# New work orders for an attention and long-convolution kernel, with some layernorm rows on GpSimd and other residual additions on VectorE

## The chip, the cores and the metric

The kernel runs on one core of a Trainium2 chip. The metric is the device time of one execution in microseconds (us); times given as "the time" are the median of several executions. The engines of the core are named as in the profile: PE is TensorE (matmul), PEld its weight loads, DVE is VectorE, ACT is ScalarE, POOL is GpSimd, and SP only issues DMAs here.

## The reference

One sequence of 2048 positions and 512 features goes through four sublayers, A, B, A, B, each with a layernorm in front and its result added to the residual stream x. A is windowed, dilated attention with 32 heads of 16 features: a position attends to itself and to seven earlier positions, two apart. B is a long convolution of the sequence with a kernel of 2048 taps for each feature, which is generated from state-space parameters.

```python
def _A_ref(x, wqkv, wo):                       # H = 32, Dh = 16, W = 8, dil = 2
    ...
    idx = pos[:, None] - off[None, :]          # off = 0, 2, ..., 14
    ...
    logits = jnp.einsum("bhsd,bhswd->bhsw", q, kg) * scale
    logits = jnp.where(mask[None, None, :, :], logits, -1e9)
    attn = _softmax(logits, axis=-1)
    o = jnp.einsum("bhsw,bhswd->bhsd", attn, vg)
    return o.transpose(...).reshape(B, S, D) @ wo
def _B_ref(u, A_re, A_im, B_re, B_im, C_re, C_im, log_dt, Dskip):
    ...
    P = jnp.exp(logdA[:, :, None] * l[None, None, :])
    K = jnp.einsum("dn,dnl,dn->dl", Cc, P, dB).real
    ...                                        # y = irfft(rfft(u, 2L) * rfft(K, 2L))[:L]
    return y + u * Dskip
x = x + _A_ref(_layernorm(x), A_wqkv, A_wo)
x = x + _B_ref(_layernorm(x), B_A_re, ..., B_Dskip)
x = x + _A_ref(_layernorm(x), A_wqkv, A_wo)
x = x + _B_ref(_layernorm(x), B_A_re, ..., B_Dskip)
```

The convolution kernel depends on the parameters alone and serves both layers. In this program it is brought into a frequency domain once, and each convolution is then a chain of two forward steps, a multiplication, and two inverse steps, all as matmuls with small transform matrices.

## The kernel before

The 2048 positions are split into 16 rows of 128, row a holding every sixteenth position from a on; x stays in SBUF as x_sb, 128 partitions by 16 rows by 512 features, in bf16. There are seven stages, by time in the profile: kernel generation together with the first layernorm, its projections and the first logits (0 to 109 us); the core of attention 0 (109 to 187); convolution 0 (187 to 237); the second front, which is the end of convolution 0, the layernorm of layer 2 and its projections (237 to 270); the core of attention 1 (270 to 360); convolution 1 (360 to 408) with the stores of the output.

The order of the instructions of PE, DVE, ACT and SP is not left to a scheduler. It is written out by hand, as strings of tokens, under a manual schedule: each token calls a small function that emits its instructions, and each engine executes what it was given in this order, waiting on semaphores where an operand is not there yet or a buffer is not free. So to move a token is to move its work on every engine that it uses. Seven strings are concerned:

- ORDERK is the order of kernel generation: 368 one-letter tokens that build the powers of the state-space poles (L1106 on DVE), the transcendental functions of ACT, the matmuls that make the convolution kernel's taps (L1264, PE), and among them the front of attention 0.
- CORE0 and CORE1 are the orders of the two attention cores, read by `core`. The tokens: v is one step of the v projection (PE matmuls L396, copied to v_ext by ACT, L398; every few steps SP copies shifted rows of v_ext by DMA, L401 and L402), q of the q projection, m a product of q and k for a row's window (DVE, L340), l its sum over the features of a head (PE, L343 to L352), x the maximum (DVE, L412), e the exponentials (ACT, L424), r the reciprocals, n the normalised weights (DVE, L443 or L446), P the product of weights and v of a row (DVE, L465, output pav), S and V its sum over the window on PE. S adds halves of pav with 64 small matmuls of 64x64 (L490), V whole ones with 32 (L480). O is the output projection (PE, L499 to L501) and the update of x by ACT (L505 or L507). b, d and a belong to the layernorm in front of the convolution: statistics, 1/sqrt, and the application to one row (`u_apply`; L195 on DVE or POOL, L193 on ACT). Digits and other letters are events: loads of w2 and of transform data, and fix-ups of the convolution kernel.
- ORDER0 and ORDER1 are the orders of the convolutions. Each token makes one tile of 128x1024 or 128x2048 elements, and its last letter says which engine takes the result out of PSUM: A for ACT, D for DVE, B for half on each. K and U are the first forward step (f1, matmuls L798, taken out by L787) of the convolution kernel and of the sequence; k and u the second (f2, L805); m the multiplication on DVE (L848, L851); y and Y half and whole tiles of the first inverse step (i1, L878, L882); z and w tiles of the second (i2). A z tile covers four rows and 256 features, a w tile eight rows and 128 features, and a v tile four rows and 128 features.
- i2 adds its result to x. Where ACT takes the tile out, PE adds x itself, by one more matmul with the identity for each row (L905, L925). Where DVE does, it adds x while it reads PSUM (L910, L929).
- KROWS gives the engine, ACT or DVE, that takes out each K tile of the second half of the kernel. ORDERF is the order of the second front: the last tiles of convolution 0, h statistics of half rows (DVE, L148), a their aggregation (L1492), p the power for 1/sqrt (ACT), n the norms of four rows (L195), T the transposes of those rows (PE, L269), E their way out of PSUM (L271), P the projection for k (PE, L280), Q that for q (L221), x and e the copies of k's shifted edges (DVE, L293).

In the second front the norm of a block of four rows is one call, which before puts all four rows on DVE:

```
def norm(b):
    la.front_apply(b, x_sb[:, b * 4:(b + 1) * 4, :], ln_end(nc, lnp, ln[b]), ["dve"] * 4)
```

In the cores the engine that applies the norm to a row is fixed by the row's number: even rows from 0 to 7 on ACT, odd ones on DVE. In layer 1 rows 8 to 15 follow behind the core on POOL, which is not under the manual order outside of kernel generation; in layer 2 rows 8 and 9 are on ACT, 10 and 11 on DVE.

The outputs leave at the end by eight stores of four rows and 256 features each (L1535, on SP), each as soon as its part of x is final.

Of the kernel before, what the change touches and what calls it, by code (L numbers as in the profile page):

```python
# [45 lines left out]
ORDERK = """
sibCCiGCsibGCiMisibsbGcCiCMibabcsMMMTMGiiMTGMaTbaisiTMbbcTTsiaTGbibsTTaiiaTbbbcMsTGaiGMaMMiGMb
lMlaMGsGWiiaMalbMyyyyTMMaaiaMtMMweMtaMMMMedTaqcMMMslMkMaqlQkiqWKMbMqMlkyHyQTkyUkUkyKTtUqtKUUppaU
qaUaUUqUxaUqaQakapxUelQekdUlpUkWKkKHxkqTlT3Tky3qxKTT3pT3pTQylyqxTkWqylxQpTkKtpzzTqzeTkqHtkxQeKUU
zktkKkUEETkeUUktKTkkUkKTUUeKkkpkxpKUxkpUEUxUKkqUxUUUUpqoUkpoxKXUQxoUkpkKXZpxXxpxZZ  # L50
"""
ORDER0 = """
KD KD KA KA KA KD KA KA KD KA KD kA KD kA KD UA UA kD UA UA UD kA UD UA UA KD
kA kD u kD kA u UA m KD u u m UA m UD UD UA UA u m KA u u m UD kA
m u kD kA m kA kD kD UA kA u kA u m yA m u m yD yA u u m YA m m
u u m m yA u m yA yA YD yD yA YD yA yA z01D yD yA
# [123 lines left out]
def ln_end(nc, pool, st):  # L180
    rstd, mean, ms = st
    nb = pool.tile(list(rstd.shape), F32, name="ln_nb")
    nc.vector.scalar_tensor_tensor(nb[:], mean, ms, rstd[:], ALU.mult, ALU.mult)
# [7 lines left out]
def ln_apply(nc, out_ap, in_ap, rstd, nb, a, eng):  # L191
    if eng == "act":
        nc.scalar.activation(out_ap, in_ap, ACT.Identity, bias=nb[:, a:a + 1], scale=rstd[:, a:a + 1])  # L193
    else:
        (nc.gpsimd if eng == "pool" else nc.vector).tensor_scalar(out_ap, in_ap, rstd[:, a:a + 1], nb[:, a:a + 1], ALU.mult, ALU.add)  # L195
# [1179 lines left out]
def kernel(  # L1375
# [104 lines left out]
    with tc.manual_schedule(engines=MAN):  # L1480
        la.front_open()
        la.front_zero()
        ln, agg, pts = {}, {}, {}
# [4 lines left out]

        def aggr(b):
            agg[b] = lnp.tile([P, 4, 2], F32, name="ln_ag")  # L1490
            for a in range(4):
# [80 lines left out]
```

## Time and profile before

| | us |
|---|---|
| median of 3 executions (lowest, highest) | 411.57 (411.03, 413.31) |
| the profiled execution | 409.99 |
| its span | 408.2 |
| DVE, ACT, PE, POOL busy in the span | 381.0, 327.0, 322.2, 55.7 |

The span goes from the first to the last instruction or transfer of the profiled execution; 1.8 us lie around it. A timeline row gives the start, the duration, the engine, the line of the kernel, the operation, output<-inputs, shapes, and how many instructions were merged into the row; in brackets how long the engine stood idle before it and which engine's result ended that. On DVE an instruction starts some 0.09 us before the one in front of it is recorded as ended, so the step from start to start is the price in a full queue: 2.20 us for a pav of 2.29, 1.14 for a copy out of PSUM of 1.22.

### The profile page before, as it was taken

To read this page: it belongs to the slowest core of one execution; us is meant where nothing else is said; L and a number is where in the kernel's file an instruction comes from. 1 tells how busy PE (TensorE), PEld (TensorE's weight loads), DVE (VectorE), ACT (ScalarE), POOL (GpSimd) and SP (SyncE) were. 2 spreads that over 40 slices of the span, in tenths; PEclk is the share of its full clock that TensorE was granted. 3 is DMA by queue.
4 is the path that set the end of the run, shared out by engine and by line. 5 is a ranking of instruction groups with operands and counts; after the bars stand their busy time and mean duration, and the time that the engine had idled before them with its cause. 6 is when DMAs were issued, how large, how long until landed. Compare 5 with 4: busy or idle time off the path is not lost.

```text
span 408.2 us, 14705 instructions
## 1 busy us (share of the span) xinstructions
PE 322.2 (79%) x6467; PEld 226.9 (56%) x6513; DVE 381.0 (93%) x478; ACT 327.0 (80%) x562; POOL 55.7 (14%) x73
## 2 busy tenths in 40 slices
PE   3000259899899888888988889999998999897794
PEld 2000127567536565656877778544466676566783
DVE  6999999999999999998899989888989999989983
ACT  7999999896456599898999978865655758889972
POOL 9300500000499200101300000000000020000000
PEclk9999999999999999999999999999999999999998
DMA  7941822132015845583245486930043027505516
GB/s 219 395 120 20 92 68 72 33 64 70 14 43 138 242 127 178 157 340 107 80 160 193 172 305 139 334 106 2 0 117 92 3 86 330 158 3 156 160 29 181
DMA packets 62322, 54.17 MB, mean 133 GB/s; under 512 B 33869, under 2 KB 50738, under 8 KB 60978
## 3 DMA queue, kind: packets, MB, share of 16 engines
q1 hardware_dynamic: 62250, 53.22, 43.1%
q8 instruction: 51, 0.84, 0.9%
q14 instruction: 13, 0.11, 0.1%
q10 hardware_dynamic: 8, 0.00, 0.0%
HBM read 30.15 MB, written 13.24 MB: 106 GB/s over the span
## 4 chain that ended last, share of the span: by engine, by line
PE 36%; ACT 15%; DVE 13%; DMA 10%; issue 6%; SPq 4%; DVEq 0%; ACTq 0%
PE pq L396 5%; PE pk L1264 5%; DVE pav L465 4%; PE pp L1202 4%; DMA v_ext<-v_ext 3%; PE pq L221 3%; ACT a1s L787 3%; PE pp L280 3%; ACT ub L864 3%; DMA w_sb<-w_dram 2%; PE L L348 2%; PE pq L501 2%; DMA kf_ring<-kf_dram 2%; PE pb L882 2%; DVE prod L340 2%
## 5 line engine op out<-in xcount | busy, mean ns | idle before, releaser
L465 DVE TENSOR_TENSOR pav<-attn,v_ext 128x4096 bf16<-128x4096 bf16 (+1 forms) x34 | 73.1, 2168 | 1.4 <-DMA v_ext<-v_ext 0.8
L340 DVE TENSOR_TENSOR prod<-qT,kT_ext 128x4096 bf16<-128x4096 bf16 x29 | 67.1, 2339 | 1.6 <-ACT qT L223 1.1
L1106 DVE TENSOR_TENSOR A_t<-A_t,pow_t 128x1024 bf16<-128x1024 bf16 (+4 forms) x46 | 38.3, 875 | 0.3
L1192 PE MATMUL pt<-ident,x_blk 128*128 128x128 bf16 x64 | 6.3, 241 | 40.0 <-DMA w_dram<-w_q 38.5
L490 PEld LDWEIGHTS <-pav 64*128 64x128 bf16 x1664 | 26.3, 95 | 14.9 <-DVE pav L465 8.0
L490 PE MATMUL po<-ident,pav 64*128 64x64 bf16 x1664 | 29.0, 190 | 6.4 <-DVE pav L465 3.6
L501 PE MATMUL pq<-wop,oT 128*128 128x512 bf16 x122 | 31.6, 379 | 2.8 <-issue 1.9
L864 ACT CAST ub<-pb 128x1024 bf16<-128x1024 f32 x32 | 32.3, 1090 | 0.1
L398 ACT CAST v_ext<-pq 128x512 bf16<-128x512 f32 x32 | 18.8, 586 | 17.0 <-PE pq L396 16.0
L805 PE MATMUL pb<-a1s,w_sb 128*128 128x64 bf16 x768 | 28.0, 193 | 5.4 <-ACT a1s L787 2.3
L396 PE MATMUL pq<-wv,xnT 128*128 128x512 bf16 x121 | 30.1, 379 | 0.6 <-ACT kgs L1272 0.3
L1202 PE MATMUL pp<-xnT,kT_ext 128*128 128x512 bf16 x87 | 25.0, 404 | 6.9 <-ACT qT L1207 2.9
L805 PEld LDWEIGHTS <-w_sb 128*128 128x128 bf16 x768 | 25.0, 98 | 8.0 <-issue 5.2
L787 DVE CAST a1s<-pb 128x1024 bf16<-128x1024 f32 x21 | 25.0, 1219 | 4.1 <-PE pb L798 4.1
L1192 PEld LDWEIGHTS <-x_blk 128*128 128x128 bf16 x64 | 4.8, 108 | 42.4 <-ACT x_blk L193 41.0
L787 ACT CAST a1s<-pb 128x1024 bf16<-128x1024 f32 x27 | 26.4, 1052 | 2.3 <-PE pb L798 2.2
L1264 PEld LDWEIGHTS <-A_t 128*64 128x64 bf16 (+1 forms) x512 | 21.8, 103 | 4.1 <-issue 0.6
L1264 PE MATMUL pk<-B_t,A_t 128*64 128x84 bf16 (+1 forms) x512 | 23.6, 201 | 0.1
L221 PE MATMUL pq<-xnT,kT_ext 128*128 128x512 bf16 x89 | 22.8, 379 | 0.5 <-issue 0.3
L176 POOL TENSOR_TENSOR ln_rstd<-ln_rstd,ln_mh 128x4 f32<-128x4 f32 x2 | 3.9, 1971 | 125.5 <-DVE ln_rstd L175 125.5
L501 PEld LDWEIGHTS <-oT 128*128 128x128 bf16 x128 | 12.4, 98 | 14.2 <-ACT oT L492 1.3
L492 ACT CAST oT<-po 128x512 bf16<-128x512 f32 x26 | 15.0, 577 | 5.7 <-PE po L490 5.6
(259 smaller groups left out, 885.0 us busy)
## 6 DMA issues: line engine op xcount, KB each, us to landing
w_sb<-w_dram SPq DMA_DIRECT2D x8, 1024.0 KB, 6.4
w_dram<-xnT SPq DMA_DIRECT2D x1, 4096.0 KB
kf_ring<-kf_dram SPq DMA_DIRECT2D x13, 256.0 KB, 4.2
kf_ring<-kf_dram SPq DMA_DIRECT2D x26, 128.0 KB, 3.9
v_ext<-v_ext SPq DMA_DIRECT2D x4, 784.0 KB, 7.4
x_blk<-in_A_x_dram SPq DMA_DIRECT2D x4, 512.0 KB, 4.5
kT_ext<-in_A_wqkv_dram SPq DMA_DIRECT2D x4, 512.0 KB, 9.9
x_sb<-in_A_x_dram SPq DMA_DIRECT2D x4, 512.0 KB, 5.2
```

The lines of the kernel that those rows point to most:

```text
L221: nc.tensor.matmul(pq[:], lhsT=self.wqk[:, dt, ft * P:(ft + 1) * P], rhs=self.xnT[:, dt, q * 512:(q + 1) * 512], start=(dt == 0), stop=(dt ...
L340: nc.vector.tensor_tensor(pr, self.qT[q][:, ft].unsqueeze(1).to_broadcast([P, W, 4, P]), kap, ALU.mult)
L396: nc.tensor.matmul(pp[:], lhsT=xnT[:, dt, a * P:(a + 1) * P], rhs=wv[:, dt, :], start=(dt == 0), stop=(dt == NDT - 1))
L465: nc.vector.tensor_tensor(pv[:, i], attn[:, n % 4].unsqueeze(2).to_broadcast([P, W, DH // parts, H]), vap, ALU.mult)
L490: nc.tensor.matmul(po[:, h, 0, i * nt + ft, :], lhsT=pvf[rows, i, w, ft * P:(ft + 1) * P], rhs=ident[rows, rows], start=(w == 0 and ft + i ...
L501: nc.tensor.matmul(pw[:], lhsT=oT[:, ftp, :], rhs=self.wo[:, ftp, :], start=False, stop=(ftp == NDT - 1))
L787: (self.nc.scalar.copy if eng == "act" else self.nc.vector.tensor_copy)(dst, src)
L805: nc.tensor.matmul(p2[:, j, :], lhsT=self.w2[:, ec * EC + j, :], rhs=a1s[:, ec * EC + j, :], start=True, stop=True)
L864: nc.scalar.copy(ub[:], p2)
L1106: return lambda: nc.vector.tensor_tensor(*args)
L1202: nc.tensor.matmul(pps[kind, b, ft][:], lhsT=la.wqk[:, dt, c:c + P], rhs=la.xnT[:, dt, b * 512:(b + 1) * 512], start=(dt == 0), stop=(dt = ...
L1264: nc.tensor.matmul(o, lhsT=lhs, rhs=Bt[:, ri, c * CH + ql].rearrange("p b g -> p (b g)"), start=(not half and j % 4 == 0 and ri == 0), sto ...
```

## The change

All seven strings are new, and three of them change what is done where:

- ORDERK holds the same 368 tokens in another order.
- CORE0 has 13 S and 3 V instead of 15 and 1; CORE1 13 S and 3 V instead of 11 and 5. There are now two letters for the norm of a row, a on DVE and f on ACT: CORE0 has 6 a and 2 f where before 4 rows were on DVE and 4 on ACT; CORE1 has 4 a and 8 f where 6 were on ACT and 6 on DVE.
- In convolution 0, one K tile goes from DVE to ACT and one U tile from ACT to DVE; KROWS has the same counts in another order. One y tile goes from DVE to ACT. The last i2 tiles before were one on DVE and seven on ACT; now they are three on DVE, one on ACT and eight v tiles (half width) on ACT.
- In the second front, the norms of blocks 0, 1 and 2 put rows 0 and 2 on GpSimd and rows 1 and 3 on DVE, six rows on GpSimd in all; block 3 stays on DVE. Two E copies change sides.
- In convolution 1, one y tile goes from DVE to ACT; the i2 tiles of DVE go from two w, three z and a half z (of a tile shared with ACT) to two w, two z and five v; those of ACT from one z, a half z and two v to three v.

```diff
 ORDERK = """
-sibCCiCGCsibGCiMisibsbGcCiCMibabcsMMMTMGiiMTGMaTbaisiTMbbcTTsiaTGbibsTTaiiaTbbbcMsTGaiGMaMMiGMb
...
+sCiibsCbiisCiiMbMCGMiMsabiMcbiasMbbCCaGiMMTsibGGTGTicMbGsbiaTbcisbbTTTMGiiTbTiMaGsaGGTMiGacMabTl
...
 ORDERF = """
-yA z00A z10A h01 h00 h10 z11A a0 z12A h11 p0 S z02A n0 a1 z03A h02 p1 T0 E01D n1 h12 a2 E00A
-z13A P01 P02 T1 E11D E10A h03 Q00 p2 P00 n2 P03 h13 P10 P12 P11 T2 a3 E20A p3 E21D n3 P13 P23
-P20 P21 T3 E31D x1 E30A P22
+yA yA z01D yA z00D yA yD h00 yA h01 YA v100A v110A v102A v013A h10 a0 p0 n0G z02A v111A v101A S v112A
+h02 h11 T0 E00A a1 E01A z13D p1 n1G v003A P03 Q00 h12 a2 P01 T1 E10A p2 P00 E11D n2G h03 P11 P12
+P13 T2 E20A h13 a3 E21D P02 p3 n3D P22 P21 P10 T3 E30D E31D P23 P20 x1
 """
 ORDER1 = """
...
-yA yA yD YD yA YA yD z03D yD yA yA w000D yA yA w010D z02D v100A v110A z11A z12D z13B
...
+YA m yA YD w000D yA yA yD yA z03D yA w010D yA yD yA z02D v103A v113D v112D v102D v110D v100A v111D v101A
 """
 CORE0 = """
-vmvvv0lvmvqxleqqmlmvrlqmvvnTlmvvxlmevmlvvrlmvvlnTqPxSePS1qmOlPr4SO2PmqS3OlnP5SP67qmOSOlP8ASOPmPb
-BOSlCSwxdeOPaSaarPODVOPnbSOPd9SEOaaPaSOPGFaaPtOSHbSOt
+vvmvvlvmvvmlvxlemvrmnlqmqvlTvqlxevqmlvmvmPvvP1rnllxS0qTmqOeVmrqP4qSl2OPPSOSOPSmPP5On3l8ml6SPCOOV
+AlxSPP7eOSrObSPn9POSdOESOPSPbDadBPfaGOtFOaaawVfHSbatO
 """
 CORE1 = """
-0m1l2ml3mvmqqqqlmlvmvvvxlqmvleqlrqmqlnTvmvvxlemvmvlvrvlmvvvlPnSTxqePSOmlqPrVOqOPmSPlnSOPOmqSlPVO
-PmbVOPlxdaVeOrPawSOPaaVOPnbSOPdSOPaSOPPaatSObStadaaaaO
+0m1l2ml3mvvqqlmmlmvqqvvllxmemqvlrnvvlmxTqqlvvmqlmvPvvvvmvqlleqVPrmxqmnqSTOePlPmSOPllSPOSPrOSnOPS
+mOSPOblxOSPPdeOSrffbVPdfwOnPfVOPSOSPafbOPSdafftOSafatO
 """
-KROWS = "ADADADAA"
+KROWS = "ADDAADAA"
...
-            def u_apply(a0, rows, eng=None):
+            def u_apply(a0, rows, eng):
...
-                             eng or ("dve" if a % 2 else "act"))
+                    ln_apply(nc, u[:, :, a, :], x_sb[:, a, :].rearrange("p (q r) -> p q r", r=4), rstd, nb, a - a0, eng)
...
+            for key, eng in (("a", "dve"), ("f", "act")):
+                ops[key] = iter([lambda eng=eng: (lambda a: u_apply(a - a % 4, (a,), eng))(next(applied))] * 12)
...
-            eng = dict(A="act", D="dve", B="both").get(tok[-1])
+            eng = dict(A="act", D="dve", B="both", G="mixed").get(tok[-1])
...
-        def norm(b):
-            la.front_apply(b, x_sb[:, b * 4:(b + 1) * 4, :], ln_end(nc, lnp, ln[b]), ["dve"] * 4)
+        def norm(b, eng):
+            la.front_apply(b, x_sb[:, b * 4:(b + 1) * 4, :], ln_end(nc, lnp, ln[b]), dict(both=["act", "dve"], mixed=["pool", "dve"]).get(eng, [eng] * 2) * 2)
```

A token H for the statistics of four whole rows (`whole_stats`) comes with the change, but none of the orders uses it.

More of the change, by code (lines that the diff above doesn't have):

```diff
@@ L46 @@
 ORDERK = """
[L47 to L50, printed above, removed]
+sCiibsCbiisCiiMbMCGMiMsabiMcbiasMbbCCaGiMMTsibGGTGTicMbGsbiaTbcisbbTTTMGiiTbTiMaGsaGGTMiGacMabTl
+MlMMMWMlaiMsiMayMwMiMybyaTMysteMMqatMaaMkeMadTkqMialKMMlQMkWMlaqMMcbqykTQHqUaUKqQaakUTyqUkyqUUpU
+KUkyUapxUxtaUpatpeUaldHQqeUqkKUkl3TT33TQkkxpWl3KxTpTxyxTylTWTpqlkyyTqpHKkzkQzxKUtkUktezUqqeUKTkT
+kQKztktkTeeKkUkUKTTkkKUUUkUxUUpxEUpkxpUkUUkpEKkKqxpkUxoxpEoKXqUokUkQUpKxpZxXxZXZ
 """
 ORDER0 = """
[L53 to L56, printed above, removed]
+KD KA KA KA KD KA KD KA KD KA KD kA kD kA kA kD UA KD UA UD kA UA kD UA KD UA
+UD UA KD kA u UD m UA KA u UD u UD m KA u kA m m UA u u kD m m u
+UA u UD kA m UA kD kA u m kA kD u kA yA m YD m u m u YA u u m u
+yA m m u yA m m YA yA yD yD
 """
@@ L59 @@
 ORDERF = """
-yA z00A z10A h01 h00 h10 z11A a0 z12A h11 p0 S z02A n0 a1 z03A h02 p1 T0 E01D n1 h12 a2 E00A
-z13A P01 P02 T1 E11D E10A h03 Q00 p2 P00 n2 P03 h13 P10 P12 P11 T2 a3 E20A p3 E21D n3 P13 P23
-P20 P21 T3 E31D x1 E30A P22
+yA yA z01D yA z00D yA yD h00 yA h01 YA v100A v110A v102A v013A h10 a0 p0 n0G z02A v111A v101A S v112A
+h02 h11 T0 E00A a1 E01A z13D p1 n1G v003A P03 Q00 h12 a2 P01 T1 E10A p2 P00 E11D n2G h03 P11 P12
+P13 T2 E20A h13 a3 E21D P02 p3 n3D P22 P21 P10 T3 E30D E31D P23 P20 x1
 """
 ORDER1 = """
-UA UD UA UD UA UD UD UA UA UD UA u UD u u m u m m UA m u UD u m u
-UA m UA u u m m u m u m u yD m u yA yA m m u m u yA m u m
-yA yA yD YD yA YA yD z03D yD yA yA w000D yA yA w010D z02D v100A v110A z11A z12D z13B
+UA UD UA UD UA UA UD UA UD UA UD u UD u u UA m u m u m UA m u m u
+UD m m UA u m u m u u yA YA u m m u yD m YA m u u m m u yA
+YA m yA YD w000D yA yA yD yA z03D yA w010D yA yD yA z02D v103A v113D v112D v102D v110D v100A v111D v101A
 """
 CORE0 = """
-vmvvv0lvmvqxleqqmlmvrlqmvvnTlmvvxlmevmlvvrlmvvlnTqPxSePS1qmOlPr4SO2PmqS3OlnP5SP67qmOSOlP8ASOPmPb
-BOSlCSwxdeOPaSaarPODVOPnbSOPd9SEOaaPaSOPGFaaPtOSHbSOt
+vvmvvlvmvvmlvxlemvrmnlqmqvlTvqlxevqmlvmvmPvvP1rnllxS0qTmqOeVmrqP4qSl2OPPSOSOPSmPP5On3l8ml6SPCOOV
+AlxSPP7eOSrObSPn9POSdOESOPSPbDadBPfaGOtFOaaawVfHSbatO
 """
 CORE1 = """
-0m1l2ml3mvmqqqqlmlvmvvvxlqmvleqlrqmqlnTvmvvxlemvmvlvrvlmvvvlPnSTxqePSOmlqPrVOqOPmSPlnSOPOmqSlPVO
-PmbVOPlxdaVeOrPawSOPaaVOPnbSOPdSOPaSOPPaatSObStadaaaaO
+0m1l2ml3mvvqqlmmlmvqqvvllxmemqvlrnvvlmxTqqlvvmqlmvPvvvvmvqlleqVPrmxqmnqSTOePlPmSOPllSPOSPrOSnOPS
+mOSPOblxOSPPdeOSrffbVPdfwOnPfVOPSOSPafbOPSdafftOSafatO
 """
@@ L527, in u_end @@
                 lns[a0] = ln_end(nc, lnp, lns[a0])
-            def u_apply(a0, rows, eng=None):
+            def u_apply(a0, rows, eng):
                 rstd, nb = lns[a0]
                 for a in rows:
-                    ln_apply(nc, u[:, :, a, :], x_sb[:, a, :].rearrange("p (q r) -> p q r", r=4), rstd, nb, a - a0,
-                             eng or ("dve" if a % 2 else "act"))
+                    ln_apply(nc, u[:, :, a, :], x_sb[:, a, :].rearrange("p (q r) -> p q r", r=4), rstd, nb, a - a0, eng)
             nc.sync.dma_start(v[0:1, 0:14, :].rearrange("p a (n c) -> p (a n) c", c=64),
@@ L556, in core @@
                 d=calls(u_end, (0,), (4,), (8,)),
-                a=calls(u_apply, *((a0, (a,)) for a0 in (0, 4) for a in range(a0, a0 + 4)), *((8, (a,), "act" if l and a < 10 else "dve") for a in range(8, 12))))
+                )
             ops = {key: iter(f) for key, f in ops.items()}
-            sums = iter(rows)
+            sums, applied = iter(rows), iter(range(12))
+            for key, eng in (("a", "dve"), ("f", "act")):
+                ops[key] = iter([lambda eng=eng: (lambda a: u_apply(a - a % 4, (a,), eng))(next(applied))] * 12)
             ops["S"], ops["V"] = (iter([lambda w=w: pv_sum(*next(sums), w)] * NA) for w in (False, True))
@@ L1482 @@
         la.front_zero()
-        ln, agg, pts = {}, {}, {}
+        ln, agg, pts, whole = {}, {}, {}, set()
         def front_pools():
@@ L1487, in front_pools, with whole_stats @@
             la.front_psum()
+        def whole_stats(b):
+            whole.add(b)
+            for a in range(4 * b, 4 * b + 4):
+                nc.vector.bn_stats(lnst["bn"][:, a, 0, :], x_sb[:, a, :])
         def aggr(b):
@@ L1491, in aggr @@
             for a in range(4):
-                nc.vector.bn_aggr(agg[b][:, a, :], lnst["bn"][:, 4 * b + a, :, :])
+                nc.vector.bn_aggr(agg[b][:, a, :], lnst["bn"][:, 4 * b + a, 0:1 if b in whole else 2, :])
         def power(b):
             ln[b] = rstd_act(nc, lnp, agg[b][:, :, 1]), agg[b][:, :, 0], -1.0
-        def norm(b):
-            la.front_apply(b, x_sb[:, b * 4:(b + 1) * 4, :], ln_end(nc, lnp, ln[b]), ["dve"] * 4)
+        def norm(b, eng):
+            la.front_apply(b, x_sb[:, b * 4:(b + 1) * 4, :], ln_end(nc, lnp, ln[b]), dict(both=["act", "dve"], mixed=["pool", "dve"]).get(eng, [eng] * 2) * 2)
         def transposes(b):
@@ L1507, in last @@
             return f
-        front = dict(S=front_pools, h=lambda g, t: half_stats(nc, lnst, x_sb, t, g), a=aggr, p=power, n=norm, T=transposes,
+        front = dict(S=front_pools, h=lambda g, t: half_stats(nc, lnst, x_sb, t, g), H=whole_stats, a=aggr, p=power, n=norm, T=transposes,
                      E=lambda b, d, eng: pts[b][d](eng), P=lambda b, ft: la.front_k(b, ["act"] * 4, (ft,)),
```

## The prediction

> **What bounds the kernel now.** I read the busy times and slices of the page first, then the stretches by stage, then VectorE's (DVE's) timeline for its marked waits, last the rows of the operations that the change moves.
>
> ```profile
> PE 322.2 (79%) x6467; PEld 226.9 (56%) x6513; DVE 381.0 (93%) x478; ACT 327.0 (80%) x562; POOL 55.7 (14%) x73
> PEclk9999999999999999999999999999999999999998
> ```
>
> DVE works 381.0 of 408.2 us, and the TensorE (PE) clock stays full, so no throttle enters the sum. But the share is a mean over stages; the stretches (start:end, length, then busy time of PE, its weight loads, DVE, ACT, POOL) separate them:
>
> ```profile
> 16.00:50.00 34.00, 1.85 (x13) 1.31 (x14) 33.71 (x57) 33.12 (x62) 5.18 (x4) 1.00 0.53 116
> 50.00:70.00 20.00, 15.03 (x148) 8.79 (x148) 19.80 (x31) 19.32 (x44) 0.00 (x0) 1.00 0.33 76
> 109.00:187.00 78.00, 69.39 (x1498) 43.06 (x1515) 77.50 (x59) 60.45 (x120) 26.75 (x16) 1.00 0.54 163
> 187.00:237.00 50.00, 43.43 (x1280) 38.02 (x1273) 46.33 (x63) 47.96 (x58) 6.06 (x8) 1.00 0.44 154
> 237.00:270.00 33.00, 32.17 (x454) 22.99 (x457) 28.35 (x82) 25.71 (x40) 0.35 (x1) 1.00 0.83 260
> 300.00:360.00 60.00, 54.88 (x1204) 38.41 (x1215) 57.36 (x56) 42.81 (x101) 2.90 (x1) 1.00 0.36 120
> 388.00:408.00 20.00, 14.29 (x358) 12.75 (x356) 12.34 (x12) 10.30 (x12) 0.00 (x0) 0.93 0.37 107
> ```
>
> Kernel generation is DVE and ACT together, both over 96% busy; core 0 is DVE alone; conv 0 is ACT (47.96 of 50); the second front is PE (32.17 of 33); core 1 is DVE with PE close behind; the tail has no full engine, it is made of hand-overs. DVE's waits of any size (bracketed: the wait in us and who ended it):
>
> ```profile
> 190.42 1.23 DVE L787 CAST a1s<-pb 128x1024 bf16<-128x1024 f32 x1 [1.58 <-PE pb L798]
> 267.27 0.69 DVE L271 COPY xnT<-pt 128x1024 bf16<-128x1024 bf16 x1 [1.78 <-PE pt L269]
> 280.66 4.50 DVE L340 TENSOR_TENSOR prod<-qT,kT_ext 128x4096 bf16<-128x4096 bf16 x2 [1.14 <-ACT qT L223]
> 306.05 1.23 DVE L412 TENSOR_REDUCE mx<-L 128x128 bf16<-128x1024 f32 x1 [0.77 <-PE L L330]
> 312.51 4.49 DVE L465 TENSOR_TENSOR pav<-attn,v_ext 128x4096 bf16<-128x4096 bf16 x2 [0.84 <-DMA v_ext<-v_ext]
> 361.56 5.75 DVE L787 CAST a1s<-pb 128x1024 bf16<-128x1024 f32 x5 [1.27 <-PE pb L798]
> 401.58 1.82 DVE L910 TENSOR_TENSOR x_sb<-pb,x_sb 128x1024 bf16<-128x1024 f32 x2 [2.04 <-PE pb L907]
> ```
>
> All its marked waits sum to 19.7 us, 3.95 of them before 16 us and almost none from there to 166. A new order can win only these, the 4.8 us from DVE's last end (403.4) to the last store (408.2), and engine work taken off a bound.
>
> **Part 1, work taken and added.** Counting DVE's instructions of the two kernels, section by section, with the step from start to start of one and the next (norm L195 0.32, cast L787 and full add L910 1.14, half tile add 0.60): core 0 has two norms more (+0.65); conv 0 and the front have six norms and one cast fewer, two full adds more (-1.93 - 1.14 + 2.28 = -0.8); core 1 two norms fewer (-0.65); conv 1 one cast, one full add and one half add fewer and five half-width adds more, each priced as the half add (-1.14 - 1.14 - 0.60 + 3.00 = +0.1). Total -0.7 us: the change doesn't live from DVE's work, so the waits decide.
>
> **Part 2, kernel generation.** The same 368 steps, DVE's queue 103.8 us end to end in both orders. From 16 us on it has no wait to lose, so an order can only keep this or spoil it. A few more neighbouring pairs now depend on each other, at about 0.12 us each: I take +0.3. Ends: -0.4 (the wait of 0.41 us on ACT at 15.92) and +1.65 (one more wait like the one at 3.22 us, 1.65 behind PE).
>
> **Part 3, core 0 to conv 0.** Before, DVE was done with its norms at 188.8 and stood 1.58 us, until PE had finished its last out_proj (started 188.78) and the first f1 (from 189.74). The new string has the last P some 2.4 us sooner and puts five of DVE's norms behind it; PE saves nothing in sum (two more V rows of 1.87 for two S of 1.11: +1.5) but has slack (69.4 of 78). Counting PE's and DVE's queues from the first product, PE comes to the first f1 2.5 us sooner and ACT to its first a1s 2.8 sooner. The eight late norms on POOL, which hold the first U (POOL ends at 198.06, U starts at 198.43), come 2 us sooner too. ACT bounds the stage behind it and gets one y tile more (0.95), so -2.8 + 0.95: I take -1.8. Ends: 0 (PE is late as before) and -2.8. The moved steps on SP (the fix-up of k_perm's halves, some 4 us later by the string; w2's load, 9.15 us to land from 170.5) are still done several us ahead of the first f1 and f2.
>
> **Part 4, second front.** PE bounds it. Tiles of i2 on DVE skip the four identity matmuls: 0.87 us of PE against 1.31 on ACT, half-width ACT tiles 0.66. Before 1 DVE + 7 ACT tiles: 0.87 + 9.17 = 10.0; after 3 + 1 + 8 half: 2.61 + 1.31 + 5.28 = 9.2, so -0.8. But DVE's first product waits for a fixed string of steps (last projection P30, e0), and PE's transposes now wait for GpSimd's two rows per block. The rows:
>
> ```profile
> L195 POOL TENSOR_SCALAR xnT<-x_sb,ln_rstd,ln_nb 128x512 bf16<-128x512 bf16 x8 | 6.1, 771 | 25.0 <-DVE ln_nb L183 24.9
> 124.43 2.35 POOL L727 TENSOR_SCALAR k_perm<-k_perm,aux 128x512 int32<-128x512 int32 x2
> 127.80 7.01 POOL L727 TENSOR_SCALAR k_perm<-k_perm,aux 128x512 int32<-128x512 int32 x2
> 264.10 1.38 DVE L195 TENSOR_SCALAR xn<-x_sb,ln_rstd,ln_nb 128x512 bf16<-128x512 bf16 x4
> ```
>
> Two rows on POOL take 1.54 us, four on DVE 1.38: 0.16 later per block, covered by the transposes still queued on PE; if that cover is gone, 3 x 0.16 = 0.5. Sum of the front: -0.3. Ends: -0.8, and +2.5 when POOL and DVE take turns (third rival).
>
> The Trainium skill speaks against this part: its page "SBUF — State Buffer", section "SBUF: two separate sides", says that a GpSimd operation excludes, for a whole instruction, a DVE operation in a two-port mode or with two SBUF inputs, and is excluded by it. The rows agree in part: the same two operations on POOL took 7.01 us beside nothing but two-input products on DVE, and 2.35 where half of that time was a reduction out of PSUM; products in that stretch took 2.69 us, elsewhere 2.29. No run here shows whether DVE's norm is in such a mode. By that rule the front is +2.5, and the sum 2.8 us higher.
>
> **Part 5, core 1.** DVE waits in it: 1.14, 0.29, 0.59, 0.77 and 0.84, 3.6 us in all. The new string has q tokens ahead of where qT held the product at 280.66; the eighth v about 4 us sooner (290.8 against 295.0), so that SP's v_ext copies (issued 295.43 before, a median 7.4 us to land) come as the first pav needs them; kf_ring's loads, behind them on SP, move along and aren't needed before conv 1. With two norms fewer, DVE could be 3.6 + 0.65 = 4.3 us sooner at its last pav. Then PE must follow: a pv_sum and an out_proj in a row start 2.23 to 2.41 us apart (347.35 to 349.58, 344.94 to 347.35), a pav 2.20, and the new tail has fewer products between the pavs to let PE catch up. Two V rows fewer give PE 2 x 0.76 = 1.5. Ends 0 and -4.3; I take about half, -2.2. The last row's chain (pav, pv_sum, out_proj, statistics, norm, U) is as long as before, so the 1.27 us at 361.56 stays.
>
> **Part 6, conv 1.** Behind the last product DVE has 11.0 us of work (10.9 before), while PE has some 13.9 instead of 16: in y tokens 9 + 1 whole (6.3) against 10 + 2 (7.9), in i2 7.6 against 8.1 by the tile times above. The waits of 0.88 and 2.04 behind PE could go, -2.9; each narrow tile costs its own hand-over (0.7 to 1.1 us of ACT's waits there). I take -1.0; ends +0.5 and -2.9. The last store is as large and its 4.8 us stay.
>
> **Sum.** +0.3 - 1.8 - 0.3 - 2.2 - 1.0 = -5.0. The profiled execution took 409.99 (span 408.2 and 1.8 around it), so 405.0; the median of the three runs, 411.57, lies 1.58 above that profile, which gives **406.6**.
>
> **Rivals.** *PE takes the gain of core 1 and the tail.* For: PE is busy 54.9 of 60 us there, and its row step of 2.23 to 2.41 exceeds a pav's 2.20; eleven rows at 0.1 to 0.2 with the V rows eat 2 us, and what waits remain shift. Against: 1.5 us less PE work. Then parts 5 and 6 give nothing: 409.99 + 0.3 - 1.8 - 0.3 + 1.58 = 409.8, no change.
>
> *Kernel generation is spoilt* (slower). DVE and ACT are both above 96% from 16 to 70 us and hand to each other, so each new wait counts whole. Price: 1.65 us each, the one at 3.22; five of them 8.2, thus 414.8. It decides from 7.0 us, the distance from 406.6 to 413.6. For: all 368 steps are rearranged, two engines without slack. Against: no step is added, and the neighbours' order is similar.
>
> *POOL and DVE take turns in the front.* Each block then takes 2 x 0.77 + 2 x 0.41 = 2.36 instead of 1.38, +0.98, three times 2.9, less 0.1 to 0.4 of cover: +2.5 in place of -0.3, so 409.4. For: the two L727 rows above, the same work at three times the price. Against: norms on POOL at 191.89 ran 0.77 us each beside DVE's casts.
>
> *The change doesn't do what it says*: the instruction counts above show that it does, so I give it nothing.
>
> **How the numbers follow.** Forecast 0.53 (its own range 403.5 to 409); take turns 0.12; PE takes it 0.16; generation spoilt 0.19. About 0.5%, 2.06 us, is what a measurement of this kernel can tell from no change: faster means under 409.5, slower over 413.6. Faster: 0.53 + 0.12 = 0.65; same 0.16; slower 0.19. For 8 in 10 the range goes down to part 5 at its good end and part 6 near its own (406.6 - 2.1 - 1.7 = 402.8), and up through the unchanged case to 413.5; what lies above is most of the spoilt generation, with little left below.
>
> **What would show it.** Right: no DVE wait of 1.58 ahead of the first a1s of conv 0; the first pav of core 1 without a DMA wait; prods at the start of core 1 without qT's 1.14; a last pav of core 1 some 4 us nearer to its first product; the end waits behind L907 under 1 us. Wrong: DVE waits between 16 and 109 us; POOL's xn rows well over 0.77 us and PE waiting at L269 for them; pavs of core 1 that wait for PE's po.

## The result, and the profile after

The changed kernel took a median of 406.37 us (405.33 to 407.00, 4 runs); before, run beside it, 411.3 us (409.94 to 413.31, 4 runs). The ratio is 0.9874, with a 95% interval of 0.9826 to 0.9922. In the later runs the kernel before took 409.5 to 409.8 us and the changed one, run again, 404.96 (ratio 0.9888). The forecast was 406.6 us, so the sum came out right. Its terms did not, and most of what follows is about that.

The stretches of the changed kernel that answer to those shown of before (start:end, length, busy time of PE, its weight loads, DVE, ACT, POOL, then the granted clock of PE, DMA share and GB/s):

```profile
16.00:50.00 34.00, 1.82 (x9) 0.97 (x10) 33.90 (x58) 33.91 (x63) 7.90 (x4) 1.00 0.57 120
109.00:187.00 78.00, 71.45 (x1411) 43.92 (x1409) 76.97 (x55) 57.86 (x117) 30.67 (x15) 1.00 0.54 162
187.00:237.00 50.00, 43.80 (x1312) 39.39 (x1313) 47.83 (x70) 49.28 (x60) 6.03 (x8) 1.00 0.47 168
237.00:270.00 33.00, 31.57 (x491) 22.70 (x483) 28.52 (x77) 25.50 (x43) 5.38 (x7) 1.00 0.71 223
300.00:360.00 60.00, 58.40 (x1397) 39.69 (x1397) 57.97 (x57) 47.43 (x107) 1.02 (x1) 1.00 0.33 114
```

Generation is as full as it was. In the last row PE has 58.4 us of 60: core 1 is now nearly full on DVE and on PE at once. How much it rose can't be read from the two rows. The profile of before lacks some of its matmul records (1204 there against 1215 weight loads, while the changed kernel has 1397 of each), and so does e3's below, which with the same code of core 1 has 56.58 us in this stretch. DVE's waits, as its timeline has them:

```profile
183.01 0.16 DVE L183 SCALAR_TENSOR_TENSOR ln_nb<-ln_s,ln_rstd 128x4 f32<-128x4 f32 x1 [0.76 <-ACT ln_rstd L154]
192.68 1.23 DVE L788 CAST a1s<-pb 128x1024 bf16<-128x1024 f32 x1 [0.89 <-PE pb L799]
265.69 1.29 DVE L271 COPY xnT<-pt 128x1024 bf16<-128x1024 bf16 x2 [0.85 <-PE pt L269]
279.45 4.49 DVE L340 TENSOR_TENSOR prod<-qT,kT_ext 128x4096 bf16<-128x4096 bf16 x2 [0.28 <-ACT qT L223]
298.08 2.29 DVE L465 TENSOR_TENSOR pav<-attn,v_ext 128x4096 bf16<-128x4096 bf16 x1 [0.19 <-DMA v_ext<-v_ext]
357.40 3.63 DVE L788 CAST a1s<-pb 128x1024 bf16<-128x1024 f32 x3 [1.27 <-PE pb L799]
387.47 1.22 DVE L930 TENSOR_TENSOR x_sb<-pb,x_sb 128x1024 bf16<-128x1024 f32 x1 [1.11 <-PE pb L928]
```

Read it against the list of before. In core 1 the five waits of 1.14, 0.29, 0.59, 0.77 and 0.84 us have shrunk to 0.28 and 0.19. At the entry of conv 0, the 1.58 us have not gone: 0.76 and 0.89 stand at two other places. The 1.27 us ahead of conv 1 are the same to the hundredth, and the 2.04 at the end became 1.11 and some smaller ones.

To see where the time went, the profile is cut at four marks that all kernels share: DVE's first product of core 0, ACT's first a1s of conv 0, DVE's first product of core 1, ACT's first a1s of conv 1. These are us between the marks, from the timelines; kernels are named here as in the experiments below.

| kernel | to first product | core 0 | conv 0 + front | core 1 | conv 1 to the end of the span |
|---|---|---|---|---|---|
| before | 109.36 | 81.85 | 78.80 | 91.11 | 47.08 |
| changed | 109.63 | 81.41 | 78.63 | 87.28 | 46.55 |
| changed, profiled again (e12) | 110.15 | 81.57 | 78.89 | 87.46 | 47.33 |
| core 1 old (e1) | 109.91 | 81.06 | 78.60 | 91.87 | 47.06 |
| core 0, conv 0, front old (e2) | 109.77 | 81.85 | 79.78 | 88.10 | 45.90 |
| front norms on DVE (e3) | 110.16 | 81.45 | 78.84 | 87.17 | 47.28 |
| last V of core 0 an S (e4) | 109.91 | 81.76 | 79.29 | 86.93 | 46.01 |
| core 1, late v (e5) | 109.61 | 80.89 | 78.94 | 90.58 | 46.88 |
| core 1, norms six and six (e6) | 110.08 | 80.89 | 79.20 | 87.72 | 46.21 |
| core 1, five V (e7) | 109.61 | 82.36 | 79.06 | 88.12 | 46.25 |
| conv 0, front old (e8) | 109.60 | 82.40 | 80.70 | 87.29 | 46.91 |
| only core 1 new (e9) | 110.16 | 82.27 | 78.97 | 88.07 | 46.43 |
| conv 1 old (e10) | 110.03 | 80.87 | 78.89 | 87.58 | 45.73 |
| core 1 without V (e11) | 110.05 | 81.18 | 78.54 | 88.59 | 47.54 |

Between the first two rows, 3.8 of the 4.7 us of span lie in core 1. The other columns move by 0.2 to 0.5 us, and rows with the same code in a stage differ by as much or more from one execution to the next. One column holds a part that no order made: the last store of the profile of before ended 4.8 us after the last write of x, those of all other runs 3.3 to 4.4 us. Up to that last write, conv 1 took 42.28 us before and 42.59 in the changed kernel.

### The profile page after: what moved, and what is told of

Read it like the earlier page. It is cut to its first block, busy times and chain, and to the rows that moved or that the text cites. A ratio compares the mean times of both kernels' runs of the same rounds, so it can differ in the third digit from the quotient of the medians.

```text
span 403.5 us, 14809 instructions
## 1 busy us (share of the span) xinstructions
PE 325.9 (81%) x6527; PEld 228.5 (57%) x6527; DVE 381.7 (95%) x475; ACT 326.2 (81%) x565; POOL 66.2 (16%) x79
## 4 chain that ended last, share of the span: by engine, by line
PE 33%; DVE 16%; ACT 11%; issue 7%; DMA 4%; POOL 0%; SPq 0%; DVEq 0%; ACTq 0%
PE pq L396 5%; DVE pav L465 5%; PE po L490 4%; PE pq L501 4%; PE pq L221 3%; DVE t L852 3%; PE pb L799 2%; DMA v_ext<-v_ext 2%; ACT ub L865 2%; PE L L352 2%; PE pb L806 2%; DVE prod L340 2%; PE pb L883 2%; DVE ln_bn L148 2%; ACT a1s L788 2%
## 5 line engine op out<-in xcount | busy, mean ns | idle before, releaser
L490 PEld LDWEIGHTS <-pav 64*128 64x128 bf16 x1664 | 26.0, 95 | 13.9 <-DVE pav L465 6.1
L501 PE MATMUL pq<-wop,oT 128*128 128x512 bf16 x128 | 32.9, 379 | 0.2 <-ACT oT L492 0.2
L490 PE MATMUL po<-ident,pav 64*128 64x64 bf16 x1664 | 29.0, 190 | 4.5 <-DVE pav L465 2.5
L1203 PE MATMUL pp<-xnT,kT_ext 128*128 128x512 bf16 x96 | 26.5, 401 | 7.0 <-ACT qT L1208 2.9
L1193 PEld LDWEIGHTS <-x_blk 128*128 128x128 bf16 x64 | 4.7, 107 | 42.2 <-ACT x_blk L193 40.6
L396 PEld LDWEIGHTS <-xnT 128*128 128x128 bf16 x128 | 11.7, 97 | 14.3 <-issue 1.7
```

The costliest lines, as they stand in the source:

```text
L396: nc.tensor.matmul(pp[:], lhsT=xnT[:, dt, a * P:(a + 1) * P], rhs=wv[:, dt, :], start=(dt == 0), stop=(dt == NDT - 1))
L490: nc.tensor.matmul(po[:, h, 0, i * nt + ft, :], lhsT=pvf[rows, i, w, ft * P:(ft + 1) * P], rhs=ident[rows, rows], start=(w == 0 and ft + i ...
L501: nc.tensor.matmul(pw[:], lhsT=oT[:, ftp, :], rhs=self.wo[:, ftp, :], start=False, stop=(ftp == NDT - 1))
L1203: nc.tensor.matmul(pps[kind, b, ft][:], lhsT=la.wqk[:, dt, c:c + P], rhs=la.xnT[:, dt, b * 512:(b + 1) * 512], start=(dt == 0), stop=(dt = ...
```

## The experiments

In the first group, whole strings go back to the old order, the norm's letter rewritten as f or a so that each row keeps its old engine.

**Core 1 old (e1).**

```diff
 CORE1 = """
-0m1l2ml3mvvqqlmmlmvqqvvllxmemqvlrnvvlmxTqqlvvmqlmvPvvvv...
+0m1l2ml3mvmqqqqlmlvmvvvxlqmvleqlrqmqlnTvmvvxlemvmvlvrvl...
```

> The changed kernel with the old order of the second attention core (old mix of S and V, six norms on ACT and six on DVE). Theory 1 (the gain sits in core 1, because DVE's waits there went): 3.8 us slower than the changed kernel's profile, 405.33 + 3.8 = 409.1; DVE waits again for qT near the start (about 1.1 us) and for DMAs of v_ext at the first pavs; first a1s of conv 1 at 361 instead of 357. Rival (the stages cover each other, and a later stage eats what an earlier one gives): at most 1.5 us slower, 406.8 or less.

Measured: 409.75 us median against 409.48 of before beside it, ratio 0.9979 (0.9953 to 1.0005); core 1 91.87 us. DVE's timeline of this run has the waits of before at their places:

```profile
280.21 4.49 DVE L340 TENSOR_TENSOR prod<-qT,kT_ext 128x4096 bf16<-128x4096 bf16 x2 [1.14 <-ACT qT L223]
301.73 2.29 DVE L465 TENSOR_TENSOR pav<-attn,v_ext 128x4096 bf16<-128x4096 bf16 x1 [0.39 <-DMA kf_ring<-kf_dram]
305.60 1.23 DVE L412 TENSOR_REDUCE mx<-L 128x128 bf16<-128x1024 f32 x1 [0.97 <-PE L L330]
312.19 4.49 DVE L465 TENSOR_TENSOR pav<-attn,v_ext 128x4096 bf16<-128x4096 bf16 x2 [0.97 <-DMA v_ext<-v_ext]
```

Theory 1 holds, the rival falls: with the old order of this one core, the six other new strings together are worth 0.2%, and the interval of that just includes nothing.

**Core 0, conv 0 and front old (e2); conv 0 and front old alone (e8).**

```diff
-KROWS = "ADDAADAA"
+KROWS = "ADADADAA"
 ORDERF = """
-yA yA z01D yA z00D yA yD h00 yA h01 YA v100A ... n0G ... n1G ...
+yA z00A z10A h01 h00 h10 z11A a0 z12A h11 p0 S z02A n0D a1 ...
```

(and ORDER0, in e2 also CORE0; e8 leaves KROWS and CORE0 as changed)

> The changed kernel with the old orders of the first core, of convolution 0 and of the second front (and the old KROWS), norms of the front on DVE. Theory 1 (by the milestones of the two profiles, these stages together gave 0.6 us): first product of core 1 0.3 us later, 270.0 against 269.67, and 0.3 to 0.7 us slower, 405.6 to 406.0 in the profile. Rival (core 1's new order needs the state in which the new front leaves PE and ACT): core 1 itself loses 1 us or more, 407 or more.

> The changed kernel with the old orders of convolution 0 and of the second front (norms on DVE, i2 one tile on DVE and seven on ACT), the new core 0 kept. The run with the old core 0 as well had core 0 0.4 us, conv 0 and front 1.1 us and core 1 0.8 us longer than the changed kernel. Theory 1 (the front's tiles do it: PE saves 0.8 us of identity matmuls, and core 1 starts with less queued on PE): conv 0 and front 0.5 to 1.1 us longer and core 1 0.8 longer here too. Rival (it came from core 0): both within 0.3 us of the changed kernel's 78.6 and 87.3.

Measured: e2 407.18 us, ratio to before 0.993 (0.9904 to 0.9956); e8 408.68, spread over 405.93 to 410.35, ratio 0.997 (0.9945 to 0.9995). By the stages neither theory was right as it stood. Conv 0 and front took 79.78 and 80.70 us, but each profile has a gap of PE in them that the profile can't put down to a wait, 0.43 us in e2 and this one in e8 (a row of PE's timeline; "issue" means that PE waited for nothing that is recorded):

```profile
246.00 0.20 PE L883 MATMUL pb<-WpJ,t 64*128 64x64 bf16 x2 [2.31 <-issue]
```

If each gap counts whole, e2 comes to 79.35 and e8 to 78.4 without it, around the 78.5 to 79.3 of the kernels with the new orders. The 0.8 us that e2 lost in core 1 is a gap of the same kind, 1.00 us at 353.87 in the last sums over the window. In e8 core 1 took 87.29, so the new front is not what lets core 1 be short.

The times say more against the old orders than the stages do. The interval of e8 lies clear of the changed kernel's (0.9826 to 0.9922, and 0.9867 to 0.991 in e12), so the old conv 0 and front behind the new core 0 do cost something. Of the 3.45 us between the two profiled executions, 2.07 lie in conv 0 and front, which is little more than the gap, and 1.0 in core 0, where e8's granted clock dropped for a while. Whether the gap is there in every execution of e8 the runs don't show. Such gaps keep their place, as the last section shows, so it may well be a price of that order.

**Front norms on DVE (e3).**

```diff
-... p0 n0G z02A ... p1 n1G v003A ... E11D n2G h03 ...
+... p0 n0D z02A ... p1 n1D v003A ... E11D n2D h03 ...
```

> The changed kernel with the six norms of the second front back from GpSimd on DVE, all else as changed. Theory 1 (DVE and GpSimd slow each other in part: two norms on DVE took 1.11 us beside GpSimd instead of 0.74, GpSimd's pair 1.68 instead of 1.45, so a block is ready about 0.4 us sooner with all four on DVE): the first product of core 1 0 to 0.9 us sooner, the time 0 to 0.9 us shorter. Rival A (full turn-taking, 2.36 us a block): 2.5 us shorter. Rival B (GpSimd relieves DVE as meant): 0.5 us or more longer.

Measured: 406.04 us, ratio 0.9879 (0.983 to 0.9929); conv 0 and front 78.84 us against 78.63 and 78.89 of the changed kernel's two profiles. So neither full turn-taking nor a relief: the step is worth nothing that can be measured. The rows of the changed kernel say how (POOL's pair, DVE's two norms beside it, and DVE's first two norms of e3, with POOL idle):

```profile
249.03 1.68 POOL L195 TENSOR_SCALAR xn<-x_sb,ln_rstd,ln_nb 128x512 bf16<-128x512 bf16 x2 [7.49 <-DVE ln_nb L183]
248.97 1.11 DVE L195 TENSOR_SCALAR xn<-x_sb,ln_rstd,ln_nb 128x512 bf16<-128x512 bf16 x2
```

```profile
249.41 0.73 DVE L195 TENSOR_SCALAR xn<-x_sb,ln_rstd,ln_nb 128x512 bf16<-128x512 bf16 x2
```

DVE's two rows take 1.11 instead of 0.73 us, POOL's two 1.68 instead of the 1.54 of two single ones. DVE saves only 0.27 us a block (1.38 for four rows, 1.11 for two), and the block is ready some 0.4 us later. PE has hardly a marked wait for it: in this stage its weight loads of L269 waited once for POOL's rows, 0.22 us, in the changed kernel, and once for DVE's, 0.25 us, in e3. The Trainium skill ("SBUF — State Buffer", section "SBUF: two separate sides") would have a GpSimd operation and a DVE operation that is in a two-port mode, or has two SBUF inputs, block each other for whole instructions; no run shows whether DVE's norm is such a one. Here the four rows were done in 1.74 us (248.97 to 250.71), not the 2.36 of one after the other. Taken one by one, DVE's first row took 0.41 us as always, its second 0.79, ending 0.15 us after POOL's first; POOL's took 0.90 and 0.79. So they do hinder each other, but not for the whole of each recorded duration.

**Last V of core 0 an S (e4).** In the changed kernel's entry to conv 0, the sum of row 14 is a V: PE needs 1.95 us for it, and the last row's sum then waits 0.44 us more for ACT's copy of it. It looked like the reason why conv 0 began no sooner.

```diff
-AlxSPP7eOSrObSPn9POSdOESOPSPbDadBPfaGOtFOaaawVfHSbatO
+AlxSPP7eOSrObSPn9POSdOESOPSPbDadBPfaGOtFOaaawSfHSbatO
```

> The changed kernel with the last V of the first core made an S (the sum over the window of row 14 in 64 small matmuls instead of 32 large ones), nothing else. Theory 1 (that V, 1.95 us on PE, delays the last row's sum and through it the first f1 of conv 0): the last row's sum starts about 0.8 us sooner (187.06 to 186.3), ACT's first a1s at 190.2 instead of 191.04, and since ACT is full in conv 0 the whole 0.8 us arrives at the first product of core 1; time 404.5 in a profile. Rival (conv 0 is held by the norms on GpSimd that gate the first U at 198.8, and these by DVE's statistics): a1s sooner, U and the end unchanged.

Measured: 405.57 us, ratio 0.9872 (0.9828 to 0.9916), no different from the changed kernel. ACT's first a1s came at 191.67, not sooner. PE's timeline has the reason:

```profile
186.78 0.23 PE L490 MATMUL po<-ident,pav 64*128 64x64 bf16 x4 [1.66 <-issue]
```

Inside the new S, PE stood for 1.66 us with no wait recorded. The S took 2.94 us, longer than the V that it replaced, so both expectations missed, and the run as it is doesn't try the V's part. The changed kernel has a gap of this kind too, in the S ahead of that V:

```profile
180.98 1.02 PE L490 MATMUL po<-ident,pav 64*128 64x64 bf16 x58 [1.23 <-issue]
```

Seven profiles have this code of core 0, one such gap and no drop of the clock there (changed, e1, e5, e6, e10, e11, e12). Their gap is 0.69 to 1.40 us long, and core 0 takes 80.87 to 81.57 us; less the gap, it is 80.17 to 80.20 in all seven. So the gap arrives at conv 0 whole. e4 less its two gaps (0.82 and 1.66 us) has 79.28, 0.9 us under those. That is about what an S saves PE (1.95 against 1.11 us): by this sum theory 1 was right about the V, and the new gap hid it. What the gaps are is taken up below.

In the second group, core 1's new order is taken apart.

**Late v (e5).**

```diff
-0m1l2ml3mvvqqlmmlmvqqvvllxmemqvlrnvvlmxTqqlvvmqlmvPvvvv...
+0m1l2ml3mvvqqlmmlmvqqvvllxmemqvlrnvlmxTqqvlvvmqlmvPvvvv...
```

> The changed kernel with the eighth v of core 1 put back by six tokens (behind l m x T q q), so that SP's copies of v_ext start later; nothing else. Theory 1 (core 1's gain is the DVE waits that went, and each of them counts whole, since DVE is full): the first pav waits for the DMA of v_ext by 2 to 4 us more, and the core from its first product to ACT's first a1s becomes longer by as much (87.3 us to 89.5 to 91). Rival (PE is the bound of core 1 and only works the queue off while DVE waits): DVE's wait appears, but the core is less than 1 us longer.

Measured: 409.59 us against 409.63 of before, ratio 0.9998 (0.9982 to 1.0015). With one token moved by six places, the time is no longer different from before:

```profile
300.88 2.29 DVE L465 TENSOR_TENSOR pav<-attn,v_ext 128x4096 bf16<-128x4096 bf16 x1 [3.23 <-DMA v_ext<-v_ext]
```

The wait grew from 0.19 to 3.23 us, and core 1 from 87.28 to 90.58: 3.0 us of new wait, 3.3 us of new time. Theory 1 holds. The profile accounts for these 3.3 us, which is also the distance of the two profiled executions; the medians, which are from other runs, differ by 3.2 (406.37) to 4.6 us (404.96), and what lies above 3.3 is open.

**Norms six and six (e6).**

```diff
-...PPdeOSrffbVPdfwOnPfVOP...
+...PPdeOSraabVPdfwOnPfVOP...
```

> The changed kernel with the first two norms of core 1 on DVE instead of ACT, which makes six and six as before. Theory 1 (DVE's work counts one for one): core 1 0.65 us longer (two steps of 0.32). Rival (PE bounds the second half of core 1): 0.2 us or less.

Measured: 405.9 us, ratio 0.9902 (0.9868 to 0.9936). Counted from the first product, the last pav ends at 81.58 us, against 80.85 and 81.04 in the changed kernel's profiles: 0.5 to 0.7 later, as two DVE norms should make it. ACT's first a1s comes only 0.3 to 0.4 later (87.72 against 87.28 and 87.46). So about half of DVE's work counts at the end, between the two theories, and it is too little to show in the time.

**Five V (e7) and no V (e11).**

```diff
-...PPdeOSrffbVPdfwOnPfVOPSOSPafb...
+...PPdeOVrffbVPdfwOnPfVOPVOSPafb...
```

(e7; e11 writes S for each of the three V of CORE1)

> The changed kernel with two late S of core 1 made V, five V as before: 1.5 us more of PE by 1.87 for a V and 1.11 for an S. Theory 1 (PE has some slack, DVE is the bound): core 1 less than 0.5 us longer, pavs without waits for PE. Rival (PE is the bound behind DVE): 0.8 to 1.5 us longer, pavs waiting for po.

> The changed kernel with the three V of core 1 made S: 2.3 us less PE by 1.87 and 1.11. Theory 1 (DVE is the bound of core 1, PE follows): core 1 within 0.4 us of 87.3. Theory 2 (PE is close behind, two V more cost 0.8 us): 0.5 to 1 us shorter. Rival (an S has twice the instructions, and PE then waits for nothing that the profile shows, as it did for 1.66 us where the first core's V became an S): longer by such a wait of 0.3 to 2 us.

Measured: e7 406.74 us, ratio 0.9928 (0.99 to 0.9956), core 1 88.12; e11 407.08 us, ratio 0.9934 (0.9909 to 0.9958), core 1 88.59. For e7 the truth is between the theories: 1.5 us more of PE cost 0.7 to 0.8, of which 0.33 shows as a wait of a pav for po. PE is close behind DVE, as the forecast feared, but it follows. e11 looks as if less PE work cost 1.2 us. Its timeline and stretches say otherwise:

```profile
323.61 2.29 DVE L465 TENSOR_TENSOR pav<-attn,v_ext 128x4096 bf16<-128x4096 bf16 x1 [1.35 <-PE po L490]
```

```profile
318.00:323.00 5.00, 5.00 (x138) 3.23 (x136) 4.24 (x2) 1.35 (x4) 0.00 (x0) 0.66 0.01 3
```

The granted clock was 0.66 in the five us ahead of that wait: PE ran slow for a short time in this execution, DVE caught up with it and waited 1.35 us. Take that off, and core 1 is 87.24 us, as in the changed kernel. So in the profile the V's of core 1 gain nothing and lose nothing, as theory 1 had it; PE also had a gap of 0.89 us without a recorded wait in an S, and DVE did not feel that one. The times don't settle it: the median is 2.1 us above that of the changed kernel beside it (e12, 404.96). The granted clock was lower in e11's four executions (0.986 to 0.995) than in e12's six (0.992 to 1.0); where it is alike, 0.995 and 0.994, both took 405.69 us.

**Only core 1 new (e9), conv 1 old (e10), the changed kernel again (e12).** e9 is the kernel before with the new CORE1; e10 the changed kernel with the old ORDER1 (its last line is shown):

```diff
 ORDER1 = """
...
-YA m yA YD w000D yA yA yD yA z03D yA w010D yA yD yA z02D v103A v113D v112D v102D v110D v100A v111D v101A
+yA yA yD YD yA YA yD z03D yD yA yA w000D yA yA w010D z02D v100A v110A z11A z12D z13B
```

> The kernel before with nothing but core 1's new order (its 8 f and 4 a norms, 13 S and 3 V); all other strings old, front norms on DVE. Theory 1 (core 1 alone carries the gain): core 1 87 us as in the changed kernel, time 3.5 to 4.5 us under before, ratio 0.989 to 0.991. Rival (the other orders are needed for it, or carry a good part): 2 us or less under before.

> The changed kernel with convolution 1 in its old order. Theory 1 (the new tail of i2 tiles saves PE and hand-overs, 0.5 us by the milestones): from ACT's first a1s to the end of the span 47.1 us as before, against 46.0 to 46.6; time 0.5 to 1 us longer than the changed kernel. Rival (run-to-run differences of the clock in the tail explain it): no difference.

> The changed kernel once more, beside the runs above. All theories: stages as in its first profile within 0.5 us, but for the waits of PE that the profile names no releaser for: if these come and go by chance, core 0, conv 0 or the tail moves by 0.3 to 1 us; if they belong to the order, the one at 181 us (1.23 us) is there again at the same place.

Measured, on one chip against the same runs of before (409.77 us): e9 407.48, ratio 0.9938 (0.992 to 0.9957); e10 404.84, ratio 0.9877 (0.986 to 0.9893); e12 404.96, ratio 0.9888 (0.9867 to 0.991).

The new order of conv 1 gains nothing that can be measured: with the old one the kernel is as fast. There is no difference, as the rival said. The four kernels with the new order and no dip of the clock there took 45.9 to 46.3 us from the first a1s to the end (e2, e4, e6, e7), the two with the old one 45.7 and 46.4 (e10, e9).

e9 is less clear: 2.3 us under before, between the rival's 2 and theory 1's 3.5. The new core 1 alone gives 0.62%, give or take 0.19; all but core 1 gives 0.21%, give or take 0.26 (e1); all seven give 1.12%, give or take 0.22. The first two make 0.83%, give or take 0.32, so it can't be told from the runs whether the parts add up or help each other. In e9's profile core 1 is 88.07 us, 3.0 shorter than before instead of 3.8, and the difference has a gap of PE in it (0.73 us at 353.84, in the last sums, where a row's way to conv 1 has no cover):

```profile
353.84 0.20 PE L490 MATMUL po<-ident,pav 64*128 64x64 bf16 x1 [0.73 <-issue]
```

## Why the prediction was right, point by point

**The bound.** That DVE's waits, not its work, decide was right. All marked waits of DVE went from 19.7 to 14.6 us. Its busy time is 381.7 us after 381.0, where part 1 had -0.7; the three pairs of norms beside GpSimd, 1.11 instead of 0.73 us each, are 1.1 us of that.

**Generation, +0.3.** Measured +0.27 between the two profiles. Four profiles of the new order have 109.60 to 109.63 us; the eight others, all with a drop of the granted clock near 60 us, have 109.77 to 110.16. One of the old order (e9) has 0.8 more than the first, without such a drop, so a difference of 0.3 us is not to be told from that between two executions. The rival of a spoilt generation didn't occur.

**Core 0 to conv 0, -1.8.** Core 0, conv 0 and front together went from 160.65 to 160.04 us, -0.6, where parts 3 and 4 had -2.1; this step failed. The prediction had "PE comes to the first f1 2.5 us sooner and ACT to its first a1s 2.8 sooner". The f1 tile behind PE's last out_proj came at 190.37 instead of 189.74, ACT's a1s at 191.04 instead of 191.21, and the first U, which was to come 2 us sooner, at 198.82 instead of 198.43. Two things were wrong. The term of 2.4 us for DVE's last pav was too large: it ended 0.5 us sooner (185.77 against 186.24), or 0.7 counted from the first product. Only three norms and a copy are gone from DVE's queue ahead of it, 1.3 us by their steps, because two of the five norms behind it are additional ones; and 0.56 us more of waits stand there, the 0.76 for ACT's ln_rstd at 183.01 against 0.20. And PE's queue had no place for the gap of 1.23 us at 180.98, which counts whole (see e4). Without it core 0 would have been 80.2 us by that sum, 1.7 us shorter than before; and the V of row 14 holds some 0.9 us more. With the old order the gap lies at 147 us, and core 0 doesn't follow its length: 0.82 and 1.31 us both go with 81.85 us, 1.36 with 82.27.

**Second front, -0.3.** About that: conv 0 and front are 0.2 us shorter. GpSimd's part is worth nothing either way (e3); the rival of full turn-taking fell, with 1.74 us for a block and not 2.36.

**Core 1, -2.2.** The mechanism was right and the size was not: -3.8. The full sum of the waits and the two norms had been 4.3, and half was taken off for PE. PE did not take its half: it was busy 58.4 of 60 us and DVE still waited for it nowhere between 285 and 350 us. The 54.9 of 60 us that stood for PE's rival came from the profile that lacks records. What PE's closeness costs is what e7 shows, about half of the 1.5 us that it adds there.

The 3.8 us are made up as follows. DVE's marked waits from the first product to the last pav fell from 3.63 to 0.46 us, and the last pav ended 3.1 us nearer to the first product (80.85 us behind it, against 83.96), not the "some 4" that were named as a sign. The other 0.7 us lie behind it: from the last pav to ACT's first a1s it was 6.43 us instead of 7.14, with 17 instructions of DVE instead of 20, where the prediction had this chain "as long as before". Of the waits, those for a DMA ahead of a pav lost 1.2 us (0.59 and 0.84 became 0.19), those for the logits 1.1 (0.29 and 0.77), that for qT 0.9. e5 shows what the transfer of v_ext costs when it comes late; it doesn't show that this transfer alone decides.

**Conv 1, -1.0.** The profiles have -0.5, but the order has no part in it that shows: with the old one e10 is as fast, and up to the last write of x conv 1 became no shorter. What became shorter is the last store, 4.8 us before and 3.9 in the changed kernel's profile. The step "the waits of 0.88 and 2.04 behind PE could go" failed: they became 1.11, 0.29, 0.22, 0.35 and others, one for each of the hand-overs of more and smaller tiles.

**The sum.** -5.0 was forecast and -4.7 of span measured: core 1's surplus of 1.6 us made up for most of the 2.0 that parts 3 and 4 (1.5) and conv 1 (0.5) lacked. That errors of this size cancelled is luck. The offset of 1.58 between profile and median also happened to be near: 406.37 is 1.04 above the profiled 405.33.

## What to carry to other kernels

Where one engine is full, sum its waits by releaser and move the issue of what ends them, not its work: one v token six places later cost 3.0 us of wait here, six norms on another engine gained nothing. A queue sum without waits is a lower bound for an order and should not be taken as its time at a place where three engines hand over to each other. And look for gaps without a releaser before a difference of a stage is put down to the order in it.

## What the runs showed of the hardware

**PE's gaps without a releaser follow the loading of its code.** Every profile has one to three gaps of over 0.4 us on PE after the first 100 us, in streams of small matmuls (the S sums of L490, i1 at L883, L431). The profile's list of queues has

```profile
q8 instruction: 51, 0.84, 0.9%
```

0.84 MB in 51 packets are 16 KB each, and PE's 13,054 recorded matmuls and weight loads make 256 for each packet. Laid beside the start and landing of these packets in the traces, all 28 such gaps of the 14 profiles end 1.25 to 1.61 us after a packet has landed; most packets land without a gap behind them. The number of packets goes with PE's instructions: 50 in e7, which has 128 fewer, 52 in e11, which has 192 more. Some of the gaps (packet's time, and when PE went on):

```
kernel   gap us   packet under way   PE goes on   after landing
before   1.31     144.5 - 145.50     146.95       1.45
changed  1.23     178.5 - 179.51     180.98       1.47
e4       1.66     184.4 - 185.43     186.78       1.35
e8       2.31     243.5 - 244.58     246.00       1.42
e9       0.73     351.4 - 352.27     353.84       1.57
e12      1.40     179.4 - 180.30     181.66       1.36
```

The gap near 181 us is in each of the eleven profiles with the new core 0, while the three with the old one have theirs at 147 us, and five profiles with the new core 1 have one near 338 us at L431 (e3, with the same order on PE, one of 0.34 us there): they belong to the place in PE's stream and not to chance, though their length varies (0.51 to 1.40 us near 181). The Trainium skill's "Runtime: NRT & Kernel Launch", section "Instruction fetch mechanics", describes code that is fetched in 16 KiB blocks of 256 instructions, at a cost that is mostly hidden; the size agrees, and if the gaps are this, the cost was not hidden here where PE ran through 128 short instructions in 1.1 us. An S has twice the instructions of a V, and the S that e4 put in place of a V got such a gap. That a fetch that comes too late is the cause was not tried by itself: it rests on the times.

**The granted clock drops to 0.50 for 3.4 us at a time.** The drop of e11 (0.66 over the five us from 318) is one from 319.5 to 322.9. Drops behind PE's last work, at the end of an execution, are left aside here. The places differ between executions of one kernel (372 us in the changed kernel's first profile, 61 and 388 in e12), but they recur: near 60 us in eight of the 14 profiles, at 388 to 391 in four, at 372 to 375 in three, at 167 in two. What one costs depends on the place. In e11 it made DVE wait 1.35 us. Near 60 us it goes with 0.2 to 0.5 us more of generation. At 167 us (e7, e8) core 0 less its gap is 81.4 and 81.9 us instead of 80.2. At 388 us, among the last tiles of conv 1, the stage was about 1.2 us longer (e1, e3, e11 and e12, 47.1 to 47.5, mean 47.3, against 45.7 to 46.4, mean 46.1, in e2, e4, e6, e7, e9 and e10). At 372 to 375 us (changed, e5, e8) no cost shows: up to the last write of x conv 1 took 42.5 to 42.6 us, like the 42.2 to 42.9 of the profiles without a drop there. A difference of one us between two profiles of this kernel is to be looked at there first.
